# GpSimd's subtractions in two pieces: weights, g of the first batch, maxima of the first pairs

## The chip, the cores and the metric

The kernel runs on one core of one Trainium2 chip. The metric is the device time of one execution in microseconds (us), the median of the runs shown. The engines are named as in the profile: PE (TensorE, matmuls; PEld its weight loads), DVE (VectorE), ACT (ScalarE), POOL (GpSimd) and SP (SyncE, which issues the loads and stores).

## What is computed

Attention over local and global tokens, and behind it a two-layer network with softplus. Batch 8, 8 heads, 512 local and 32 global positions, head dimension 64; the network has 4608 tokens, 512 inputs and 2048 hidden features.

```python
k_all = concat([k_g, k_l]); v_all = concat([v_g, v_l])
out_g = softmax(scale * q_g @ k_all.T) @ v_all
s_ll  = where(|i - j| <= 32, scale * q_l @ k_l.T, -1e9)
out_l = softmax(concat([scale * q_l @ k_g.T, s_ll])) @ v_all
x = concat([out_g, out_l]) as (tokens, heads * dim)
h = x @ w_in
g = max(h, 0) + log1p(exp(-|h|))
out = g @ w_out
```

The weights arrive as 64-bit floats, and the products of the network are made with 32-bit values split in two parts.

## The kernel before

**Two parts.** The attention works on 32 pairs of heads (4 pairs to a batch of the network's input). Pairs 0 to 5 go through a first loop (L674 to L698) step by step: scores on PE, row maximum on DVE (L171, L172), exponential on ACT (L174), reciprocal of the sum on DVE (L180, L181), weighing on POOL (`weigh0`, L186), transposes on PE, copies by ACT (L213, L214), values on PE, and the split of the result (L238, L239). In that loop each step also prepares one weight tile. Pairs 6 to 31 are worked in pieces (`pieces`, L424) that are laid between the network's items of the batch before: `scores`, `block_maxima`, `maxima`, `probs`, `totals`, `values`, `normalise`. Of these, pairs 6, 7 and 8 (m below WIDE, L36) lie in or before batch 0.

**The network.** `moe_items` (L520) lists, batch after batch, `hpart` (PE: four 128-row blocks of x against a weight tile wi, three products each: high by high, low weight by high, high by low), `act` (L545) and `opart` (PE: g against wo, again three products). `act` makes g = e from h: three ACT activations (L548 to L550), one DVE instruction that reads PSUM (L551, called e below), an ACT copy to the high part gh (L554) and a POOL subtraction that leaves the low part gl (L555). `opart` for row block t reads gh twice and gl once, columns 128 t to 128 t + 127 (L563).

**A weight tile.** `abs_w` (ACT, L488) scales the upper words, `bits_w` (DVE, L495, L497 and L500, each from the one before) puts the 32-bit value together, `halves_w` makes the high half by an ACT copy (L505) and the low half by a POOL subtraction (L506). There are 32 such tiles, 16 of each kind (wi and wo). The first 16 are prepared in the first loop (W_PRE, L42).

**The maxima.** `probs` (L371) spreads the block maxima with four DVE transposes (L375) and subtracts them from the scores of both heads on POOL: five subtractions per pair (L378), of 160 and 352 columns a head in the first half of the scores and 32, 384 and 96 in the second. ACT's exponential of that half (L380) follows, then DVE's sums (L384), `totals` with small instructions on 32 partitions (L357 to L361, L389, L390, L393), and at the end `normalise` (L415 to L420).

**Order.** Each engine takes its instructions in the order of its queue. The tile framework draws that order at compile time from a simulated time line (L773), with the program's order as priority and waits where data need them. In the first loop `keep` and `note` (L157, L478) chain the instructions of ACT and DVE, and `mm` those of PE, in the program's order; after it (`tight = False`, L699) PE's chain remains, and DVE's weight work is only kept behind the maxima (L496). POOL's order is left to the framework throughout. Weights after the first 16 are prepared as batch 0 goes on (`weights`, L644, from L704 and L710).

Of the kernel before, what the change touches and what calls it, by code (L numbers as in the profile page):

```python
# [8 lines left out]
F32 = mybir.dt.float32  # L9
# [4 lines left out]
ALU = mybir.AluOpType  # L14
# [21 lines left out]
WIDE = 9  # L36
# [17 lines left out]
def windows(ap2d, start, stride, count, width):  # L54
    base = ap2d[:, start:start + width]
    return bass.AP(base.tensor, base.offset, [list(base.ap[0]), [stride, count], [1, width]])
# [3 lines left out]
def moe_over_global_local_attention(  # L60
# [11 lines left out]
    nc = tc.nc  # L72
# [22 lines left out]
    for o, w, base, sign in ((32, 32, 0, 1), (64, 32, -96, -1), (96, 128, 32, 1), (96, 128, 32, -1)):  # L95
        r = mask0[:, 0, 1, o:o + w]
# [274 lines left out]
    def probs(m, g):  # L371
        s, e = st["s", m], st["e", m]
        mb = pl.tile([P, 2, 416], F32, tag="mb", name=f"mb{m}_{g}", bufs=2)
        for o, k, n in (((0, 1, 8), (256, 7, 5)), ((0, 10, 6), (192, 14, 6)))[g]:
            nc.vector.transpose(mb[:, :, o:o + 32 * n].rearrange("p h (s k) -> p h s k", k=32),  # L375
                                windows(e, k, 21, 2, n).unsqueeze(3).to_broadcast([P, 2, n, 32]))
        for o, q, w in (((0, 0, 160), (160, 64, 352)), ((512, 64, 32), (544, 0, 384), (928, 288, 96)))[g]:
            nc.gpsimd.tensor_tensor(s[:, :, o:o + w], s[:, :, o:o + w], mb[:, :, q:q + w], op=ALU.subtract)  # L378
        s = s[:, :, 512 * g:512 * g + 512]
        nc.scalar.activation(s, s, AF.Exp, scale=0.125)  # L380
        if g == 0:
            st["zt", m] = pl.tile([P, 348], F32, tag="zt", name=f"zt{m}", bufs=2)
            nc.gpsimd.memset(windows(st["zt", m], 0, 36, 3, 4), 0.0)
        nc.vector.tensor_reduce(windows(st["zt", m], 4 + 16 * g, 36, 2, 16), s.rearrange("p h (b k) -> p h b k", k=32),  # L384
                                axis=AX.X, op=ALU.add, apply_transpose=True)
# [38 lines left out]
    def pieces():  # L424
        def piece(*fs):
            def go():
                for f in fs:
                    f()
            return go
        ps = []  # L430
        for m in range(M0, M):
            g0, g1, mx, tot, val = SLOTS.get(m, (None, None, 12 * m + 5, 12 * m + TOT, 12 * m + VAL))
            for g, slot in ((0, g0), (1, g1)) if m in SLOTS else ():
                fs = [lambda m=m, g=g: scores(m, g)]
                if m + 1 < M:
                    fs += [lambda m=m, p=p: load(m + 1, p) for p in ((0,), (1, 2))[g]]
                ps.append((slot, piece(*fs)))
            ps.append((mx, piece(lambda m=m: maxima(m), *[lambda m=m, q=q: probs(m, q) for q in range(2)])))
            ps.append((tot, lambda m=m: totals(m)))
            fs = [lambda m=m: values(m), lambda m=m: normalise(m)]  # L440
            if m + 2 < M:
                fs.append(lambda m=m: load_v(m + 2))
            ps.append((val, piece(*fs)))
        ps.sort(key=lambda t: t[0])
        return ps
# [32 lines left out]
    def note(what, i):  # L478
        if tight:
            keep(what, i)  # L480
        return i
# [9 lines left out]
    def bits_w(kind, k, a):  # L491
        t = raws.pop((kind, k))
        lo32, hi32 = t[:, :, 0], t[:, :, 1]

        i = nc.vector.tensor_scalar(a, a, 3, None, op0=ALU.logical_shift_left)  # L495
        note("dve", i) if tight else after(i, "maxima")  # L496
        note("dve", nc.vector.scalar_tensor_tensor(a, hi32, SIGN, a, op0=ALU.bitwise_and, op1=ALU.bitwise_or))  # L497

        r = lo32 if k < NF - 1 else pl.tile([P, 512], I32, tag="mb", name=f"wlast{kind}", bufs=2)
        note("dve", nc.vector.scalar_tensor_tensor(r, lo32, 29, a, op0=ALU.logical_shift_right, op1=ALU.bitwise_or))  # L500
        return r.bitcast(F32)

    def halves_w(kind, k, r):
        (wi if kind == "wi" else wo)[k] = o = pl.tile([P, 2, 512], F32R, tag=f"{kind}{k}", name=f"{kind}{k}", bufs=1)
        note("act", nc.scalar.copy(o[:, 0], r))  # L505
        nc.gpsimd.tensor_tensor(o[:, 1], r, o[:, 0].bitcast(F32), op=ALU.subtract)  # L506

    def split_w(kind, k):
        halves_w(kind, k, bits_w(kind, k, abs_w(kind, k)))
# [10 lines left out]
    def moe_items():  # L520
# [24 lines left out]
        def act(b, f):  # L545
            ph = g.pop(("ps", b, f))
            e = pl.tile([P, 512], F32, tag="e", name=f"e{b}_{f}", bufs=2)
            nc.scalar.activation(e, ph, AF.Abs)  # L548
            nc.scalar.activation(e, e, AF.Exp, scale=-1.0)  # L549
            nc.scalar.activation(e, e, AF.Ln, bias=one)  # L550
            nc.vector.scalar_tensor_tensor(e, ph, 0.0, e, op0=ALU.max, op1=ALU.add)  # L551
            gh = pl.tile([P, 512], F32R, tag="gh", name=f"gh{b}_{f}", bufs=3)
            gl = pl.tile([P, 512], F32R, tag="gl", name=f"gl{b}_{f}", bufs=3)
            nc.scalar.copy(gh, e)  # L554
            nc.gpsimd.tensor_tensor(gl, e, gh.bitcast(F32), op=ALU.subtract)  # L555
            g[b, f] = (gh, gl)

        def opart(b, f, t):
# [33 lines left out]
        for i, (b, f) in enumerate(tiles):  # L592
            if f == 0 and b > 0:
                items.append((b, 0, 0, lambda b=b: [split_x(b, j) for j in range(4)]))
            if 0 < b < B - 1:
                if f == 0:
                    h = iter(range(NF))
                    for what in ORDER:
                        if what == "H":
                            f = next(h)  # L600
                            items.append((b, 2, 0, lambda b=b, f=f: hpart(b, f, (0, 1))))
                            items.append((b, 2, 0, lambda b=b, f=f: (hpart(b, f, (2, 3)), act(b, f))))
                        elif what == "O":
                            second(done, b)
                            second(done + 1, b)
                            done += 2
                        else:
                            m = next(wide, None)
                            if m:
                                items.append((b, 0, 0, lambda m=m: both_scores(m)))  # L610
                continue
# [3 lines left out]
            w = 0 if b else 4 * f  # L615
            items.append((b, 2, w and w + 2, lambda b=b, f=f: hpart(b, f, (0, 1))))
            items.append((b, 2, w and w + 4, lambda b=b, f=f: (hpart(b, f, (2, 3)), act(b, f))))
            behind = 1 if (b, f + 1) not in tiles or (f == 0 and b > 0) else 2
            upto = halves.index(tiles[i - behind] + (0,)) + (2 if tiles[i - behind][0] < B else 1) if i >= behind else 0
# [54 lines left out]
    for k in range(-2, n + 2):  # L674
        stage(k + 2, 0)

        while k >= n - 2 and pcs[0][0] < min(12 * M0 + 3 * (k - n + 3), START):
            pcs.pop(0)[1]()
        if k == 0:
            key_masks()  # L680
        for at, m, load_0 in ((5, 4, load_q0), (8, 4, load_v0), (8, 5, load_q0), (11, 5, load_v0)):
            if k == at + 1:
                load_0(m)
        if held:
            r = bits_w(*held)
        stage(k + 2, 1)
        stage(k - 2, 5)
        stage(k - 2, 6)
        stage(k, 3)
        stage(k, 4)  # L690
        stage(k + 2, 2)
        if held:
            halves_w(*held[:2], r)
            held = None
        if -1 <= k and wk[1] < W_PRE:
            held = order_w[wk[1]]
            held += (abs_w(*held),)
            wk[1] += 1  # L698
    tight = False  # L699
    if held:  # L700
        halves_w(*held[:2], bits_w(*held))
# [75 lines left out]
```

## Time and profile before

| | us |
|---|---|
| median of 3 runs (984.21 to 985.17) | 984.22 |
| the profiled execution | 983.79 |
| its span | 982.0 |
| PE busy | 946.7 |
| DVE busy | 638.3 |
| ACT busy | 502.8 |
| POOL busy | 434.4 |

The span runs from the first to the last instruction in the trace; the rest of an execution's time lies around it. Busy times are sums over one engine's instructions; the recorded end of matmuls is modelled, so a busy PE is not PE at its best. A row of the order of time gives the start, the length, the engine, the source line, the operation, the tiles (written <- read), the shape and how many were merged; in square brackets the idle time of the engine before it, and what ended it. A row with the line L127 is any matmul, since all go through `mm`; h, o, s and so on tell which. The recorded length of an instruction includes any time that it stands at its engine before its work starts.

### The profile page before, as it was taken

Reading aid. Unit: us, or ns where it says so; the run is one execution under the profiler, and the core shown is the slowest. Engines: PE = TensorE matmul, PEld = TensorE weight load, DVE = VectorE, ACT = ScalarE, POOL = GpSimd, SP = SyncE. Lnnn points to the kernel's source line nnn. Section 1 sums busy time; section 2 is a strip of 40 time slices with the busy share of each in tenths; the row PEclk is TensorE's granted clock in tenths of the full one; section 3 lists DMA queues with packets and bytes.
Section 4 is the critical chain, followed back from the end, with each engine's and each line's share of the span. In section 5 each row is a group of like instructions: output and inputs, shape, how many; then the busy total and the mean of one; then the engine's idle time right before and its main releaser. Section 6 shows DMA issues by size and latency. Waiting matters only on the chain.

```text
span 982.0 us, 14339 instructions
## 1 busy us (share of the span) xinstructions
PE 946.7 (96%) x5236; PEld 763.9 (78%) x5239; DVE 638.3 (65%) x1295; ACT 502.8 (51%) x890; POOL 434.4 (44%) x580
## 2 busy tenths in 40 slices
PE   6797898999999999999999999999999999999998
PEld 3575676778888888888888888888888888888896
DVE  6888959776677866776677677776777676211211
ACT  5786656554445544454464444544454446444553
POOL 5655746534444444253444444444434444222221
PEclk9899899999999999999999999999999999999999
DMA  9824222120112211121112111121112100100000
GB/s 356 319 78 163 85 77 72 43 89 27 43 50 79 64 49 49 50 88 38 50 27 96 37 50 50 55 87 49 50 49 76 50 17 17 50 1 1 12 33 22
DMA packets 34327, 66.21 MB, mean 67 GB/s; under 512 B 7632, under 2 KB 11472, under 8 KB 34256
## 3 DMA queue, kind: packets, MB, share of 16 engines
q1 hardware_dynamic: 33440, 65.19, 20.2%
q8 instruction: 41, 0.67, 0.3%
q14 instruction: 30, 0.25, 0.1%
q10 hardware_dynamic: 816, 0.10, 0.1%
HBM read 55.84 MB, written 9.44 MB: 66 GB/s over the span
## 4 chain that ended last, share of the span: by engine, by line
PE 84%; DVE 9%; ACT 3%; issue 1%; POOL 1%; POOLq 0%; ACTq 0%; DVEq 0%
PE o L127 37%; PE h L127 36%; PE s_ps L127 5%; PE v_ps L127 5%; DVE wbitswi L497 1%; ACT e L174 1%; DVE wiraw L500 1%; DVE wbitswo L497 1%; DVE sums L171 1%; PE s L127 1%; DVE woraw L500 1%; DVE wbitswi L495 1%; DVE wbitswo L495 1%; PE s0g L127 0%; DVE zt L393 0%
## 5 line engine op out<-in xcount | busy, mean ns | idle before, releaser
L127 PE MATMUL h<-xh,wi 128*128 128x512 f32 (+1 forms) x1152 | 347.8, 386 | 10.6 <-DVE e L551 10.6
L127 PE MATMUL o<-wo,gh 128*128 128x512 f32 x1088 | 345.6, 399 | 0.0
L555 POOL TENSOR_TENSOR gl<-e,gh 128x512 fp32r<-128x512 f32 x136 | 180.1, 1324 | 266.2 <-ACT gh L554 235.4
L127 PEld LDWEIGHTS h<-xh,wi 128*128 128x128 f32 x1152 | 214.3, 190 | 57.5 <-DVE e L551 12.3
L127 PEld LDWEIGHTS o<-wo,gh 128*128 128x128 f32 x1088 | 200.3, 188 | 48.2 <-POOL wo L506 0.2
L127 PE MATMUL h<-xl,wi 128*128 128x512 f32 (+1 forms) x576 | 220.6, 383 | 0.0
L127 PE MATMUL o<-wo,gl 128*128 128x512 f32 x544 | 214.6, 394 | 0.7 <-POOL gl L555 0.7
L551 DVE SCALAR_TENSOR_TENSOR e<-h,e 128x512 f32<-128x512 f32 x136 | 92.7, 682 | 183.0 <-ACT e L550 164.7
L548 ACT ACTIVATE e<-h 128x512 f32<-128x512 f32 x136 | 81.0, 596 | 223.4 <-PE h L127 222.9
L378 POOL TENSOR_TENSOR s<-s,mb 128x320 f32<-128x320 f32 (+4 forms) x130 | 138.4, 1097 | 73.3 <-DVE mb L375 73.3
L554 ACT CAST gh<-e 128x512 fp32r<-128x512 f32 x136 | 83.9, 617 | 117.4 <-DVE e L551 117.4
L127 PEld LDWEIGHTS h<-xl,wi 128*128 128x128 f32 x576 | 109.5, 190 | 22.8
L127 PEld LDWEIGHTS o<-wo,gl 128*128 128x128 f32 x544 | 102.3, 188 | 24.8 <-POOL gl L555 1.0
L550 ACT ACTIVATE e<-e,one 128x512 f32<-128x512 f32 x136 | 98.4, 724 | 3.9
L384 DVE TRANSPOSE_TENSOR_REDUCE zt<-s 128x32 f32<-128x1024 f32 x52 | 64.6, 1243 | 48.6 <-ACT s L380 48.5
L549 ACT ACTIVATE e<-e 128x512 f32<-128x512 f32 x136 | 85.9, 631 | 2.9
L380 ACT ACTIVATE s<-s 128x1024 f32<-128x1024 f32 x52 | 55.1, 1059 | 31.1 <-POOL mt L318 25.9
L333 DVE TRANSPOSE_TENSOR_REDUCE mt<-s 128x32 f32<-128x1024 f32 x52 | 64.7, 1244 | 5.0 <-ACT s L322 3.4
L127 PEld LDWEIGHTS s_ps<-raw 64*128 64x128 f32 x728 | 54.6, 187 | 11.4 <-issue 8.9
L354 POOL COPY mt<-mt 32x75 f32<-32x75 f32 x78 | 19.0, 244 | 94.5 <-DVE mt L333 92.4
L127 PE MATMUL s_ps<-raw 64*128 64x192 f32 (+3 forms) x728 | 60.2, 308 | 0.5
L375 DVE STREAM_TRANSPOSE mb<-mt 128x512 f32<-128x512 f32 (+1 forms) x104 | 52.6, 562 | 0.7
(131 smaller groups left out, 860.7 us busy)
## 6 DMA issues: line engine op xcount, KB each, us to landing
raw<-in_qk SPq DMA_DIRECT2D x52, 272.0 KB, 2.8
v<-in_v SPq DMA_DIRECT2D x26, 384.0 KB, 3.1
out<-ot SPq DMA_DIRECT2D x34, 256.0 KB, 2.2
wiraw<-in_w_in SPq DMA_DIRECT2D x16, 512.0 KB, 9.0
woraw<-in_w_out SPq DMA_DIRECT2D x16, 512.0 KB, 8.2
raw<-in_qk SPq DMA_DIRECT2D x26, 224.0 KB, 3.3
v<-in_v SPq DMA_DIRECT2D x6, 512.0 KB, 7.2
raw<-in_qk SPq DMA_DIRECT2D x6, 416.0 KB, 8.4
```

The lines of the kernel that those rows point to most:

```text
L127: order["pe"] = after(nc.tensor.matmul(*a, **k), "pe").ins
L333: order["scores"] = nc.vector.tensor_reduce(windows(st["mt", m], 4 + 16 * g, 36, 2, 16), s.rearrange("p h (b k) -> p h b k", k=32), axis=A ...
L375: nc.vector.transpose(mb[:, :, o:o + 32 * n].rearrange("p h (s k) -> p h s k", k=32), windows(e, k, 21, 2, n).unsqueeze(3).to_broadcast([P ...
L378: nc.gpsimd.tensor_tensor(s[:, :, o:o + w], s[:, :, o:o + w], mb[:, :, q:q + w], op=ALU.subtract)
L380: nc.scalar.activation(s, s, AF.Exp, scale=0.125)
L384: nc.vector.tensor_reduce(windows(st["zt", m], 4 + 16 * g, 36, 2, 16), s.rearrange("p h (b k) -> p h b k", k=32), axis=AX.X, op=ALU.add, a ...
L548: nc.scalar.activation(e, ph, AF.Abs)
L549: nc.scalar.activation(e, e, AF.Exp, scale=-1.0)
L550: nc.scalar.activation(e, e, AF.Ln, bias=one)
L551: nc.vector.scalar_tensor_tensor(e, ph, 0.0, e, op0=ALU.max, op1=ALU.add)
L554: nc.scalar.copy(gh, e)
L555: nc.gpsimd.tensor_tensor(gl, e, gh.bitcast(F32), op=ALU.subtract)
```

## The change

Three kinds of POOL subtraction are issued as two instructions where it was one, each over half of the elements, in the same place of the program: the low half of every weight tile (columns 0 to 255 and 256 to 511), gl of batch 0 (the same columns), and, for pairs 6, 7 and 8, the subtractions of the maxima that are over 160 columns wide (352 and 384), one head at a time.

```diff
         for o, q, w in (((0, 0, 160), (160, 64, 352)), ((512, 64, 32), (544, 0, 384), (928, 288, 96)))[g]:
-            nc.gpsimd.tensor_tensor(s[:, :, o:o + w], s[:, :, o:o + w], mb[:, :, q:q + w], op=ALU.subtract)
+            for h in (slice(0, 1), slice(1, 2)) if m < WIDE and w > 160 else (slice(0, 2),):
+                nc.gpsimd.tensor_tensor(s[:, h, o:o + w], s[:, h, o:o + w], mb[:, h, q:q + w], op=ALU.subtract)
...
         note("act", nc.scalar.copy(o[:, 0], r))
-        nc.gpsimd.tensor_tensor(o[:, 1], r, o[:, 0].bitcast(F32), op=ALU.subtract)
+        for c in (slice(0, 256), slice(256, 512)):
+            nc.gpsimd.tensor_tensor(o[:, 1, c], r[:, c], o[:, 0, c].bitcast(F32), op=ALU.subtract)
...
             nc.scalar.copy(gh, e)
-            nc.gpsimd.tensor_tensor(gl, e, gh.bitcast(F32), op=ALU.subtract)
+            for c in (slice(0, 256), slice(256, 512)) if b == 0 else (slice(0, 512),):
+                nc.gpsimd.tensor_tensor(gl[:, c], e[:, c], gh[:, c].bitcast(F32), op=ALU.subtract)
```

## The prediction

> **What bounds the kernel now.** I read the page first (span, chain by engine), then busy time by stage, then the order of time on DVE and POOL, one beside the other, where PE is not full.
>
> ```profile
> span 982.0 us, 14339 instructions
> PE 84%; DVE 9%; ACT 3%; issue 1%; POOL 1%; POOLq 0%; ACTq 0%; DVEq 0%
> ```
>
> PE holds 84% of the chain that ended last, DVE 9%, POOL 1%. So POOL's own time is worth almost nothing; the question is what POOL does to DVE. The stages, with PE's busy time and granted clock (PEclk):
>
> ```profile
> core 0: us, PE busy (x) PEld busy (x) DVE busy (x) ACT busy (x) POOL busy (x), PEclk, DMA share, GB/s
> 0.00:87.00 87.00, 68.14 (x550) 51.81 (x551) 67.84 (x134) 63.10 (x183) 49.51 (x94) 0.94 0.66 240
> 87.00:101.00 14.00, 7.44 (x26) 5.66 (x25) 13.70 (x21) 7.63 (x14) 10.90 (x11) 0.75 0.30 115
> 101.00:166.00 65.00, 63.94 (x305) 50.40 (x308) 53.36 (x87) 40.30 (x63) 42.80 (x38) 0.98 0.27 88
> 166.00:172.00 6.00, 2.77 (x8) 1.89 (x7) 5.93 (x8) 3.53 (x6) 2.30 (x3) 0.75 0.00 1
> 206.00:982.00 776.00, 771.17 (x4193) 627.95 (x4191) 470.53 (x1003) 368.51 (x593) 309.22 (x416) 1.00 0.15 47
> ```
>
> From 206 on PE is busy 771.17 of 776 us, and the change leaves that part's instructions alone (pairs from 9 on, batches from 1 on): it only moves as a block. PE's slack is in the attention steps (0 to 87), in 87 to 101 and in 166 to 172; in the last two DVE is busy 13.70 of 14.00 and 5.93 of 6.00 us, so DVE is the bound there. Why DVE is so full shows when one of its weight instructions is seen alone and beside a POOL subtraction:
>
> ```profile
> 16.51 0.69 DVE L500 SCALAR_TENSOR_TENSOR wiraw<-wiraw,wbitswi 128x512 int32<-128x512 int32 x1
> 25.02 1.67 DVE L500 SCALAR_TENSOR_TENSOR wiraw<-wiraw,wbitswi 128x512 int32<-128x512 int32 x1
> 24.42 1.73 POOL L506 TENSOR_TENSOR wi<-wiraw,wi 128x512 fp32r<-128x512 f32 x1
> ```
>
> The same L500 takes 0.69 us alone and 1.67 us here, and ends at 26.69, 0.54 after the POOL subtraction's end at 26.15: it does its work after POOL is through. A stall of 0.98 us, set by what is left of one POOL instruction. Its length is what the change cuts.
>
> **The change, part by part.** It adds 54 POOL instructions: 32 for the weights (16 of each kind), 16 for g of batch 0, 6 for the maxima of pairs 6, 7 and 8 (widths 352 and 384, by head). Nothing is moved to another engine or queue, no DMA is added; what reads both pieces (ACT's exponential, PE's products with a whole row) now waits for the second. What a piece costs, from undisturbed POOL groups later in the run (mean ns after the bar):
>
> ```profile
> L555 POOL TENSOR_TENSOR gl<-e,gh 128x512 fp32r<-128x512 f32 x101 | 130.1, 1288 | 187.0 <-ACT gh L554 160.8 <-issue 26.2
> L378 POOL TENSOR_TENSOR s<-s,mb 128x768 f32<-128x768 f32 x22 | 40.8, 1855 | 0.0
> L378 POOL TENSOR_TENSOR s<-s,mb 128x64 f32<-128x64 f32 x22 | 7.1, 323 | 0.0
> ```
>
> (1855 - 323) / 704 columns is 2.18 ns a column, and 323 - 64 x 2.18 leaves 0.18 us per instruction; 512 columns come to 1.30, and the row says 1.288. So 256 columns take an estimated 0.74 us: the first half is there 0.55 earlier than the whole, and the second, with some overlap of neighbours, about 0.14 later. 54 x 0.14 is 7.6 us more of POOL, hidden behind POOL's idle time (49.51 of 87 us busy in the attention); where POOL is full it makes its consumers 0.14 late each.
>
> Whether DVE gets in between two pieces decides everything. Three tiny copies met a run of back-to-back POOL subtractions:
>
> ```profile
> 116.98 1.32 POOL L506 TENSOR_TENSOR wo<-woraw,wo 128x512 fp32r<-128x512 f32 x1
> 118.26 1.31 POOL L506 TENSOR_TENSOR wi<-wiraw,wi 128x512 fp32r<-128x512 f32 x1
> L393 DVE COPY zt<-zt x3: 1146/1255/1268, 115.9 to 118.3; 32x21 f32<-32x21 f32 x3
> ```
>
> Each of the three copies took about one POOL instruction (1146 to 1268 ns), and three copies were done in the time of three subtractions: one DVE instruction slips in at each border. So the pieces halve a stall. But the row also shows the price: a DVE instruction that depends on the one before arrives while the next piece already holds the way. Where a stalled DVE instruction is followed by another that POOL can block, the second half blocks that one, and I count nothing. Where it is followed by one that POOL does not block, 0.55 is gained. The reductions are of that kind (L384 below ran beside five subtractions and took no longer than the mean of all 52; I take L171 and L333 to be alike):
>
> ```profile
> 190.10 6.26 POOL L378 TENSOR_TENSOR s<-s,mb 128x320 f32<-128x320 f32 x5 [2.55 <-DVE mb L375]
> 194.05 1.25 DVE L384 TRANSPOSE_TENSOR_REDUCE zt<-s 128x32 f32<-128x1024 f32 x1
> L384 DVE TRANSPOSE_TENSOR_REDUCE zt<-s 128x32 f32<-128x1024 f32 x52 | 64.6, 1243 | 48.6 <-ACT s L380 48.5
> ```
>
> *Attention, 0 to 87.* Three blocked L500 (the first at 25.02 above, the last at 34.32) are followed by L180, L181 and a reduction: gains. ACT limits what they are worth:
>
> ```profile
> 34.32 1.67 DVE L500 SCALAR_TENSOR_TENSOR woraw<-woraw,wbitswo 128x512 int32<-128x512 int32 x1
> 28.59 0.45 ACT L174 ACTIVATE e<-s,sums 128x224 f32<-128x224 f32 x1 [0.55 <-DVE sums L172]
> 37.60 0.82 DVE L172 TENSOR_SCALAR sums<-sums 128x4 f32<-128x4 f32 x1
> 71.83 0.67 ACT L505 CAST wi<-wiraw 128x512 fp32r<-128x512 f32 x1
> 76.16 0.66 ACT L505 CAST wo<-woraw 128x512 fp32r<-128x512 f32 x1 [1.13 <-DVE woraw L500]
> ```
>
> ACT idled 0.55 us for DVE in such a step, so a gain of 0.55 is just used up; I take 0.45 for each of the three, 1.35. L172 at 37.60, which takes about 0.17 when free, releases the exponentials: 0.55. At 76.16 ACT waited 1.13 for a blocked L500: 0.55. At 71.83 it did not wait, and the same stall there gives nothing. Blocked L497 and L495, each followed at once by its dependent, give nothing. Sum 2.45. Bounds: 0 if every second half finds a victim; 5.5 if all ten stalls that I count in this stage's order of time gave 0.55.
>
> *The first pair's maxima, 93 to 101.*
>
> ```profile
> 94.50 1.96 DVE L497 SCALAR_TENSOR_TENSOR wbitswi<-wiraw,wbitswi 128x512 int32<-128x512 int32 x1
> 96.85 2.29 DVE L500 SCALAR_TENSOR_TENSOR wiraw<-wiraw,wbitswi 128x512 int32<-128x512 int32 x1
> 101.17 1.22 PE L127 MATMUL h<-xh,wi 128*128 128x512 f32 x2 [6.73 <-DVE e L551]
> ```
>
> Against 0.69 alone these lost 1.27 and 1.60, and PE waited 6.73 us for the L551 behind them. Halves of 704 and 768 are about 0.77 and 0.84 shorter, 1.6 at best; but L497, L495, L500 follow each other here, all blockable, so most second pieces find a victim. I take 0.7, between -0.3 (the extra instructions alone) and 1.6.
>
> *PE's second gap, 166 to 172.*
>
> ```profile
> 151.44 1.53 DVE L497 SCALAR_TENSOR_TENSOR wbitswo<-woraw,wbitswo 128x512 int32<-128x512 int32 x1
> 152.89 1.32 DVE L418 TENSOR_TENSOR xa<-xa,lap 128x64 f32<-128x64 f32 x1
> 159.59 1.26 DVE L361 COPY zt<-zt 32x6 f32<-32x6 f32 x1
> 161.37 1.29 DVE L389 TENSOR_SCALAR zt<-zt 32x42 f32<-32x42 f32 x1
> 169.63 1.22 PE L127 MATMUL h<-xh,wi 128*128 128x512 f32 x2 [3.23 <-DVE e L551]
> 169.63 5.49 PE h L127 x12
> 178.29 2.79 PE h L127 x12
> ```
>
> Three small instructions were held over a microsecond each behind g's and the weights' subtractions, and DVE, busy without a break, reached L551 3.23 us late. Halving gives 3 x 0.55 and about 0.35 for the L497 at 151.44: 2.0. Then the gap is 1.2. After it PE's first twelve matmuls took 5.49 instead of 2.79: a restart at low clock (0.75 in this stage), 2.70 lost. What a gap of 1.2 us costs the trace does not show. The neighbour on one side is this one, on the other the gap of 0.73 at 205.39 (below), with twelve per 2.75 after it:
>
> ```profile
> 205.39 0.50 PE L127 MATMUL o<-wo,gl 128*128 128x512 f32 x1 [0.73 <-POOL gl L555]
> 207.98 5.50 PE h L127 x24
> ```
>
> So between 0 and 2.70; I take half, 1.35 saved. Together 3.35, between 0 and 3.23 + 2.70 = 5.93. [...]
>
> *The end of batch 0.* In that last pair PE waited 0.73 for gl; its first two row blocks (L563) need columns 0 to 255 only, so if the wait is by region they start 0.55 earlier, less 0.14 for the weight ahead in POOL's queue: 0.4, between -0.14 and 0.73.
>
> Sum: 2.45 + 0.7 + 3.35 + 0.4 = 6.9 us. The profiled execution took 983.79 us (its span 982.0 and 1.79 around it), 0.43 under the median of 984.22: 983.79 - 6.9 + 0.43 = **977.3 us**.
>
> **The rivals.**
>
> *Hand-over.* Every second piece finds a victim and DVE's total stays; only the stall before ACT's 1.13 wait and the end of batch 0 gain, with L172: 0.55 + 0.55 + 0.4 = 1.5, time 982.7. For it: L393's three stalls in a row. Against: L384, L171 and L333 stand behind several of the stalls.
>
> *Another order (slower).* The order in each queue is drawn at compile time from estimated durations (L773), and after L699 little pins weights against e. New POOL durations can put an L551 behind one more weight chain on DVE between 101 and 169. It decides from the point where L551 comes late enough for PE to restart cold: then a second gap like 166's, 3.23 + 2.70 = 5.93, comes on top, and 166's stays. 984.2 - (2.45 + 0.7 + 0.4) + 5.9 = 986.6. For it: PE has such a gap already. Against: the change alters POOL by a tenth of a microsecond per instruction.
>
> *POOL keeps the way over both pieces.* Then each stall is 0.14 longer; some 20 stalls between 0 and 169 make 2.8, time 987.0. Against: the three copies. [...]
>
> **How the numbers follow.** Forecast 0.57, hand-over 0.22, other order 0.15, POOL keeps the way 0.06. A measurement of this kernel tells about 0.2%, 2 us, from no change. Hand-over is mostly within it (0.18 of 0.22); from the forecast 0.02 falls within. Faster 0.57 - 0.02 + 0.04 = 0.59, same 0.18 + 0.02 + 0.01 = 0.21, slower 0.15 - 0.01 + 0.06 = 0.20. Upper bounds together (5.5 + 1.6 + 5.93 + 0.73 = 13.8) would give 970.5, unlikely all at once: I end the range at 971.5. Upward it takes in hand-over and part of the order case, to 985.5; about 0.2 is left out above and below. The forecast's own range is 973 to 981.
>
> **What would show it.** Right: blocked L500 near 1.1 instead of 1.67; the 20-odd weight stalls halved; PE's gap at 166 under 1.5 with the twelve matmuls after it near 2.8; PE's first h about 2.5 earlier. Wrong: L497 and L500 both stalled where one was (hand-over); a new PE gap ended by e L551 (order); stalls of 1.8 (POOL keeps the way). It is wrong too if ACT, not DVE, paces the steps up to 87 after all.

## The result and the profile after

The changed kernel took 977.94 us (median of four runs, 975.84 to 979.50), the kernel before 984.22 in the runs beside it: a ratio of 0.9937, 95% interval 0.9925 to 0.9949, 6.3 us faster. The predicted time was 977.3. The execution profiled is the slowest of the four, 979.5 us.

The busy times on the page of after:

```profile
PE 948.4 (97%) x5239; PEld 765.0 (78%) x5239; DVE 630.0 (64%) x1295; ACT 502.4 (51%) x890; POOL 451.1 (46%) x634
```

DVE is busy 8.3 us less than before (638.3), POOL 16.7 us more (434.4). DVE's 96 weight instructions (L495, L497 and L500 before, L496, L498 and L501 after) have 3.5 of the 8.3: they took 81.7 us before and take 78.2 after. Before, 23 of them took over 1.0 us, the longest 2.29; after, 32 do, the longest 1.48. So the stalls are shorter, but there are more of them. Here is the order of time of after, DVE in the attention, at the place where the prediction counted "three blocked L500 ... gains" (below L488 the line numbers of after are one to three higher: L500 is now L501):

```profile
22.06 0.18 DVE L181 RECIPROCAL sums<-sums 128x4 f32<-128x4 f32 x1
22.65 1.09 DVE L171 TENSOR_REDUCE sums<-s 128x4 f32<-128x896 f32 x1 [0.41 <-PE s L127]
25.30 1.12 DVE L501 SCALAR_TENSOR_TENSOR wiraw<-wiraw,wbitswi 128x512 int32<-128x512 int32 x1
26.34 0.71 DVE L180 TENSOR_SCALAR sums<-sums 128x4 f32<-128x4 f32 x1
27.08 0.18 DVE L181 RECIPROCAL sums<-sums 128x4 f32<-128x4 f32 x1
31.76 0.18 DVE L181 RECIPROCAL sums<-sums 128x4 f32<-128x4 f32 x1
35.61 0.14 DVE L180 TENSOR_SCALAR sumsg<-sumsg 128x1 f32<-128x1 f32 x1
35.78 0.16 DVE L181 RECIPROCAL sumsg<-sumsg 128x1 f32<-128x1 f32 x1
```

and before:

```profile
22.20 0.18 DVE L181 RECIPROCAL sums<-sums 128x4 f32<-128x4 f32 x1
26.61 0.16 DVE L180 TENSOR_SCALAR sums<-sums 128x4 f32<-128x4 f32 x1
26.80 0.18 DVE L181 RECIPROCAL sums<-sums 128x4 f32<-128x4 f32 x1
31.50 0.18 DVE L181 RECIPROCAL sums<-sums 128x4 f32<-128x4 f32 x1
36.08 0.16 DVE L181 RECIPROCAL sumsg<-sumsg 128x1 f32<-128x1 f32 x1
```

L501 now stands 1.12 us where L500 stood 1.67, as forecast. But the next instruction, L180, an addition on four columns, takes 0.71 instead of 0.16: the second piece holds it. L181 behind it takes 0.18 in both. From L181 to L181 the second of these steps took 4.70 us before (26.80 to 31.50) and 4.68 after (27.08 to 31.76): what the first piece gives, the second takes. The third step is another matter: its L180 adds to one column only (sumsg), took 0.14 beside the second piece, and the step went from 4.58 us (31.50 to 36.08) to 4.02 (31.76 to 35.78), as forecast. The first got longer, 4.60 to 5.02, of which 0.41 is DVE's wait for PE's scores at 22.65.

PE at the gap of batch 0, after:

```profile
167.15 0.73 PE L127 MATMUL h<-xh,wi 128*128 128x512 f32 x2 [2.31 <-DVE e L553]
167.46 1.16 DVE L498 SCALAR_TENSOR_TENSOR wbitswi<-wiraw,wbitswi 128x512 int32<-128x512 int32 x1
168.65 1.13 DVE L501 SCALAR_TENSOR_TENSOR wlastwi<-wiraw,wbitswi 128x512 int32<-128x512 int32 x1
169.78 0.69 DVE L553 SCALAR_TENSOR_TENSOR e<-h,e 128x512 f32<-128x512 f32 x1
```

and before, the two weight instructions behind the gap:

```profile
169.95 1.71 DVE L497 SCALAR_TENSOR_TENSOR wbitswi<-wiraw,wbitswi 128x512 int32<-128x512 int32 x1
171.69 1.66 DVE L500 SCALAR_TENSOR_TENSOR wlastwi<-wiraw,wbitswi 128x512 int32<-128x512 int32 x1
```

The gap is 2.31 us where it was 3.23, and PE goes on at full clock (1.00 from 166.18 to 169.59 us). In this profile, though, PE is slow elsewhere: most of its products of o0g and the first h behind them run at half clock (0.50 from 84.26 to 91.08 us), so the first h starts at 87.85, later than before (87.09). One profile of each kernel is therefore not enough to say where 6 us went; the experiments gave twelve more.

**One table for all.** Four events cut every profile in the same way: PE's first product, DVE's first L333 (pair 6), the first e (L551 before), and the e that ends the gap at 166 (the 11th). In after and before:

```profile
3.92 0.91 PE L127 MATMUL s<-mask,ident 128*128 128x448 bf16 x2 [3.92 <-DVE mask L101]
78.62 1.23 DVE L333 TRANSPOSE_TENSOR_REDUCE mt<-s 128x32 f32<-128x1024 f32 x1
99.16 0.68 DVE L553 SCALAR_TENSOR_TENSOR e<-h,e 128x512 f32<-128x512 f32 x1
166.41 0.68 DVE L553 SCALAR_TENSOR_TENSOR e<-h,e 128x512 f32<-128x512 f32 x1
```

```profile
3.92 0.90 PE L127 MATMUL s<-mask,ident 128*128 128x448 bf16 x2 [3.92 <-DVE mask L101]
79.46 1.24 DVE L333 TRANSPOSE_TENSOR_REDUCE mt<-s 128x32 f32<-128x1024 f32 x1
100.44 0.68 DVE L551 SCALAR_TENSOR_TENSOR e<-h,e 128x512 f32<-128x512 f32 x1
168.90 0.68 DVE L551 SCALAR_TENSOR_TENSOR e<-h,e 128x512 f32<-128x512 f32 x1
173.27 0.68 DVE L551 SCALAR_TENSOR_TENSOR e<-h,e 128x512 f32<-128x512 f32 x1
```

A is from the first product to L333 (after 78.62 - 3.92 = 74.70), B to the first e, C to the 11th e, D1 to the 12th e, D2 to the end of PE's last product. "Slow" counts the stretches of 3.41 us at half clock in 12 to 23 and in 39 to 50 us. The last two columns are medians and ratios, each to the runs of the kernel before that stood beside it (their medians lie between 983.78 and 984.41). The stretches come from one execution each, and that isn't always a typical one: the profile of weights alone is its fastest run (977.40 against a median of 980.58), that of after its slowest (979.50 against 977.94).

| kernel | A | slow | B | C | D1 | D2 | median us | ratio (interval) |
|---|---|---|---|---|---|---|---|---|
| before | 75.54 | 1, 2 | 20.98 | 68.46 | 4.37 | 804.10 | 984.22 | |
| after | 74.70 | 2, 2 | 20.54 | 67.25 | 3.37 | 803.26 | 977.94 | 0.9937 (0.9925 to 0.9949) |
| after again | 73.16 | 2, 1 | 20.38 | 66.72 | 3.37 | 803.34 | 977.41 | 0.9934 (0.9922 to 0.9946) |
| weights alone | 71.51 | 1, 0 | 20.84 | 66.38 | 3.36 | 804.40 | 980.58 | 0.9947 (0.9933 to 0.9960) |
| g alone | 76.10 | 2, 2 | 21.05 | 67.15 | 3.83 | 803.01 | 981.38 | 0.9962 (0.9950 to 0.9975) |
| maxima alone | 76.08 | 2, 2 | 20.56 | 69.40 | 4.37 | 804.42 | 984.48 | 0.9999 (0.9990 to 1.0008) |
| after, maxima whole | 72.93 | 1, 1 | 20.84 | 67.36 | 3.36 | 802.99 | 978.34 | 0.9944 (0.9931 to 0.9956) |
| after without L180 | 71.43 | 1, 1 | 20.53 | 66.94 | 3.37 | 803.30 | 977.12 | 0.9919 (0.9906 to 0.9933) |
| before without L180 | 74.68 | 1, 2 | 21.02 | 68.61 | 4.38 | 804.14 | 982.76 | 0.9986 (0.9977 to 0.9995) |
| weights in quarters | 72.21 | 1, 2 | 19.13 | 67.87 | 5.31 | 802.56 | 978.73 | 0.9950 (0.9936 to 0.9963) |
| extra products, batch 0 | 72.80 | 1, 1 | 20.42 | 67.14 | 3.36 | 803.96 | 978.13 | 0.9941 (0.9930 to 0.9953) |
| extra products, attention | 71.36 | 1, 0 | 20.55 | 66.96 | 3.36 | 803.28 | 975.89 | 0.9922 (0.9909 to 0.9936) |
| first weights in quarters | 70.58 | 1, 1 | 19.08 | 67.78 | 3.37 | 803.57 | 975.17 | 0.9914 (0.9900 to 0.9927) |
| three together | 68.34 | 1, 0 | 19.32 | 67.52 | 3.37 | 803.24 | 972.15 | 0.9876 (0.9859 to 0.9892) |

### The profile page after: what moved, and what is told of

Its sections match the earlier page's. It is cut to its first block, busy times and chain, and to the rows that moved or that the text cites. A ratio compares the mean times of both kernels' runs of the same rounds, so it can differ in the third digit from the quotient of the medians.

```text
span 977.7 us, 14397 instructions
## 1 busy us (share of the span) xinstructions
PE 948.4 (97%) x5239; PEld 765.0 (78%) x5239; DVE 630.0 (64%) x1295; ACT 502.4 (51%) x890; POOL 451.1 (46%) x634
## 4 chain that ended last, share of the span: by engine, by line
PE 85%; DVE 8%; ACT 2%; issue 2%; POOL 1%; DMA 1%; SPq 0%; POOLq 0%; ACTq 0%; DVEq 0%
PE o L127 37%; PE h L127 36%; PE s_ps L127 6%; PE v_ps L127 5%; DVE wbitswo L498 1%; ACT e L174 1%; DVE sums L171 1%; PE s L127 1%; DMA woraw<-in_w_out 1%; DVE woraw L501 1%; DVE wbitswo L496 1%; PE t L127 1%; DVE wbitswi L498 0%; DVE e L553 0%; PE s0g L127 0%
## 5 line engine op out<-in xcount | busy, mean ns | idle before, releaser
L558 POOL TENSOR_TENSOR gl<-e,gh 128x512 fp32r<-128x512 f32 (+1 forms) x152 | 181.8, 1200 | 265.9 <-ACT gh L556 234.8
L379 POOL TENSOR_TENSOR s<-s,mb 128x320 f32<-128x320 f32 (+6 forms) x136 | 139.7, 1062 | 73.0 <-DVE mb L375 73.0
L551 ACT ACTIVATE e<-e 128x512 f32<-128x512 f32 x136 | 85.9, 631 | 2.9
L333 DVE TRANSPOSE_TENSOR_REDUCE mt<-s 128x32 f32<-128x1024 f32 x52 | 64.7, 1245 | 6.2 <-ACT s L322 4.6
```

The costliest lines, as they stand in the source:

```text
L333: order["scores"] = nc.vector.tensor_reduce(windows(st["mt", m], 4 + 16 * g, 36, 2, 16), s.rearrange("p h (b k) -> p h b k", k=32), axis=A ...
L379: nc.gpsimd.tensor_tensor(s[:, h, o:o + w], s[:, h, o:o + w], mb[:, h, q:q + w], op=ALU.subtract)
L558: nc.gpsimd.tensor_tensor(gl[:, c], e[:, c], gh[:, c].bitcast(F32), op=ALU.subtract)
```

## The experiments

### The three parts alone, and one taken away

Weights alone, g alone, maxima alone: the other two loops of the diff go back to the whole subtraction. "After, maxima whole" takes only the maxima's pieces out:

```diff
-            for h in (slice(0, 1), slice(1, 2)) if m < WIDE and w > 160 else (slice(0, 2),):
-                nc.gpsimd.tensor_tensor(s[:, h, o:o + w], s[:, h, o:o + w], mb[:, h, q:q + w], op=ALU.subtract)
+            nc.gpsimd.tensor_tensor(s[:, :, o:o + w], s[:, :, o:o + w], mb[:, :, q:q + w], op=ALU.subtract)
```

> Only the weights' subtractions in two pieces; those of g and of the maxima whole as before. Theory A (a piece halves one stall of DVE, the rest finds the next instruction of DVE that POOL can hold; what shortens the run is the gap at 166 and the cold matmuls behind it): the attention's 0.8 us is all here (PE's first o0g product of pair 0 at about 83.5 instead of 84.3), and of the small stalls ahead of 166 those behind weights are halved (L418, part of L361), so the gap at 166 is about 2.7 instead of 3.23; the restart behind it warm or cold decides between 982.5 and 980. Theory B (the new order of the queues makes the gain): about 984, unless the order of e L551 changes. Theory C (the first half reaching PE and ACT earlier makes the gain): 983.5, since no reader of a weight takes the halves one by one. Forecast 981.5, ratio 0.997.

> Only g of batch 0 in two pieces. Theory A: nothing before 87 (no g there); the stalls behind g between 101 and 169 halve, the gap at 166 shrinks by 0.5 to 1 and the restart behind it may stay warm: 984.2 less 0.5 to 3.5, about 982.5, ratio 0.998. Theory C (the halves reach PE sooner): the 0.73 wait for gl at 205 goes down by 0.4 and the gaps at 108.70 and 127.61 (0.41 and 0.26) go: 983.2. Theory B: 984.2 plus or minus 2, with an exchange in DVE's order before 169.

> Only the maxima of pairs 6 to 8 by head. Theory A: the stalls at 94.50 and 96.85 (1.96 and 2.29) become about 1.2 each, but L495, L497 and L500 follow one another and the second pieces hold those: e L551 0.4 us earlier, 983.8; nothing at 166. If the victims were not there, 1.6 us: 982.6. Theory B: 984.2 plus or minus 2. Forecast 983.8, ratio 0.9995.

> The changed kernel with the maxima of pairs 6 to 8 whole again: weights and g of batch 0 in two pieces. The pieces of the maxima made the stretch from the first L333 to the first e 0.5 us shorter (20.5 against 21.0), but in the kernel with them alone the stretch up to the gap at 166 was 0.9 longer (69.40 against 68.46), with some of DVE's queue in another order. Theory A (the order made that, the pieces gain): here 0.5 slower than the changed kernel, 978. Rival (the extra pieces of POOL cost it in batch 0): 0.4 faster, 977.1. The stretch from the first e to 166 tells: 67.0 or 66.4 (weights alone had 66.38).

The weights give most: A, C and D1 all shrink (C by 2.1, D1 by 1.0). g gives C 1.3, D1 0.5, and D2 1.1. In the profile of g alone, DVE and ACT take their instructions in the same order as before up to 206 us (PE's order is the program's), and it is still 0.4% faster: a gain needs no other order. In the changed kernel DVE's order does differ from before's in several places between 104 and 158 us; what that is worth there wasn't tried apart. The two waits for gl at the end of batch 0, first of weights alone, then of g alone, show the piece reaching PE sooner:

```profile
198.70 0.50 PE L127 MATMUL o<-wo,gl 128*128 128x512 f32 x1 [0.74 <-POOL gl L556]
```

```profile
203.10 0.50 PE L127 MATMUL o<-wo,gl 128*128 128x512 f32 x1 [0.18 <-POOL gl L556]
```

0.56 us less, as forecast by the size of a half (0.55). The maxima are worth 0.4 to 0.5 in B wherever they are split (20.98 to 20.54, 20.84 to 20.5), and nothing measurable in all: alone, C grew by 0.9. In that profile DVE takes a few instructions at 150 to 158 us in another order than before (two of `normalise` ahead of a weight's first instruction, and an e ahead of a reduction of `totals`). But the changed kernel and every other kernel here with the maxima's pieces has the same exchange, and those without these pieces don't. With the weights and g split in halves too, C is 66.7 to 67.25 with it and 67.36 without ("after, maxima whole"). So the expectation that this order made the loss isn't borne out, and why C grew with the maxima alone stays open; one profile for each is thin evidence, and the two times (978.34 and 977.4 to 977.9) can't be told apart. By the medians the three parts come to 3.8 + 3.0 + 0 = 6.8 us, against 6.3 and 6.5 together; with intervals of over 1 us either way these can't be told from a plain sum. In C they don't add: 2.1 and 1.3 alone, 1.1 for weights and g together.

### L180: does the second piece find a victim?

```diff
-        keep("dve", nc.vector.tensor_scalar(t[:, 2, 0:n], t[:, 2, 0:n], 1e-9, None, op0=ALU.add))
         keep("dve", nc.vector.reciprocal(t[:, 0, 0:n], t[:, 2, 0:n]))
```

taken out of the changed kernel, and out of the kernel before (this addition is left out; each sum holds the exponential of its row's maximum, about 1).

> The changed kernel without the addition of 1e-9 to the attention's sums (L180): the sums go to the reciprocal as they are. Theory A: L180 takes the second piece's stall in four of the attention's steps (0.71 instead of 0.16); without it the reciprocal L181 comes next, which POOL didn't hold, and each of these steps ends some 0.5 to 0.7 us earlier, as far as ACT allows: PE's first o0g product at 81.5 to 82.5 instead of 83.5, the run 1 to 2 us faster than the changed kernel, about 976.5. Rival (ACT or the loads pace the steps, L180 was only where the waiting showed): L181 or the next instruction starts no earlier, under 0.3 us gained, 977.7. Rival (the reciprocal is held as well once it stands behind the piece): L181 takes 0.7 instead of 0.16 and nothing is gained.

> The kernel before without the addition of 1e-9 to the attention's sums (L180), all subtractions whole. Theory A (L180 matters in the changed kernel because the second piece hits it): here L180 takes 0.16 us in the crowded steps and runs after POOL is through, so its absence gives 0.2 us a step at most, under 2 us in all before 87 and less at the end: 982.5 to 984. Rival (the step is simply shorter by an instruction with a wait, in either kernel): as much gained as the changed kernel gained by it, 0.8 to 1.8 us: 982.4 to 983.4. The stalls of L500 tell more than the time: 1.67 each in both theories; L181's end in a blocked step, against the start of the step before it.

The reciprocal has line 180 in both. After without the addition:

```profile
21.86 0.17 DVE L180 RECIPROCAL sums<-sums 128x4 f32<-128x4 f32 x1
24.08 2.32 POOL L507 TENSOR_TENSOR wi<-wiraw,wi 128x256 fp32r<-128x256 f32 x2
25.72 0.16 DVE L180 RECIPROCAL sums<-sums 128x4 f32<-128x4 f32 x1
34.47 0.15 DVE L180 RECIPROCAL sumsg<-sumsg 128x1 f32<-128x1 f32 x1
```

Before without it:

```profile
21.95 0.17 DVE L180 RECIPROCAL sums<-sums 128x4 f32<-128x4 f32 x1
35.35 0.15 DVE L180 RECIPROCAL sumsg<-sumsg 128x1 f32<-128x1 f32 x1
```

Reciprocal to reciprocal, the three steps take, in us:

| kernel | first | second | third | sum |
|---|---|---|---|---|
| before | 4.60 | 4.70 | 4.58 | 13.88 |
| after | 5.02 | 4.68 | 4.02 | 13.72 |
| before without L180 | 4.40 | 4.63 | 4.37 | 13.40 |
| after without L180 | 3.86 | 4.92 | 3.83 | 12.61 |

So the pieces alone gave 0.16 in three steps; without the addition they give 0.79. In whole subtractions the addition costs 0.48 in the three steps, in pieces 1.11. The gain isn't in every step, though: it shows in the first, while the second got longer (4.92), with a wait of 0.44 for ACT in it. What the second piece holds is plainer. Four additions on four columns (at 26.34, 31.02, 65.92 and 70.59 in after) met a second piece, and each took 0.70 or 0.71. The two reciprocals on four columns that met one, at 25.72 (POOL is at its two pieces from 24.08 to 26.40) and at 67.16, took 0.16 and 0.17: the piece holds the addition, not the reciprocal. In A at like slow stretches the addition is worth 0.9 us before (75.54 to 74.68) and 1.4 after (72.80 and 72.93 to 71.43). The whole time doesn't separate the theories: by the ratios 1.4 us were gained before, and 1.5 to 1.8 after, with intervals of about 1 us either way.

### Four pieces

```diff
-        for c in (slice(0, 256), slice(256, 512)):
+        for c in (slice(128 * u, 128 * u + 128) for u in range(4)):
```

for all weights, and then for the first 17 only, those up to about 100 us (`w = 128 if len(wi) + len(wo) <= 17 else 256`).

> The weights' subtractions in four pieces of 128 columns (32 weights x 2 more instructions), the rest as in the changed kernel. A piece of 128 is 0.46 us by 0.18 + 128 x 2.18 ns (an estimate from the rows of the subtractions), four are 1.84 against 1.48 for two. Theory A (one DVE instruction per border, each further border finds the next one): L500 0.85 us at a border, then L180, and no second victim once L181 and the reduction come; the step gets no shorter than now by more than 0.25, while POOL gets 0.36 longer for each weight: 977 to 979, not faster than the changed kernel. Rival (the stall is all that counts, and shorter is always better): 2 x 0.28 less on each stalled instruction: 975.5.

> The first 17 weights (those up to 100 us) in four pieces, the others in two, the rest as in the changed kernel. With four pieces throughout, the stretch from the first L333 to the first e (L553) took 19.13 us against 20.4 to 20.5, the attention at the same clock was 1.5 to 2 us shorter, but from the first e to the one that ends the gap at 166 it took 67.87 against 66.7 to 67.25, and the rest 807.87 against 806.7, with PE waiting 1.94 us for a late gl. Theory A (quarters gain where DVE is late, and lose where POOL is): both gains stay and both losses go, 975 to 975.8. Rival (batch 0 swallows what comes earlier, since its weights and x come no earlier): 977.5, with a longer stretch from the first e to 166.

All weights in quarters, the order of time of DVE, then of POOL and PE at 166 to 170:

```profile
25.03 0.84 DVE L501 SCALAR_TENSOR_TENSOR wiraw<-wiraw,wbitswi 128x512 int32<-128x512 int32 x1
25.79 0.43 DVE L180 TENSOR_SCALAR sums<-sums 128x4 f32<-128x4 f32 x1
...
165.99 2.58 POOL L508 TENSOR_TENSOR wo<-woraw,wo 128x128 fp32r<-128x128 f32 x4 [3.28 <-ACT wo L506]
168.53 1.42 POOL L558 TENSOR_TENSOR gl<-e,gh 128x256 fp32r<-128x256 f32 x2
169.31 0.50 PE L127 MATMUL o<-wo,gl 128*128 128x512 f32 x1 [1.94 <-POOL gl L558]
```

Both stalls shrink again (1.12 to 0.84, 0.71 to 0.43). My expectation of "not faster" was right for the whole (978.73) and too low for the parts: B fell by 1.3 us, A is 72.21 with three slow stretches. A part of what gave it back is in the last rows: four pieces of a wo take POOL 2.58 us, gl stands behind them, and PE waits 1.94 us for gl. The 12th e came late too (D1 5.31 instead of 3.37); whether POOL's length or another order of ACT and DVE made that wasn't separated. With quarters only up to 100 us the gains stay and D1 is 3.37 again: 975.17, the forecast being 975 to 975.8. C is 67.8 to 67.9 in both, 0.5 to 1.2 longer than with halves; why wasn't found. In both DVE and ACT take batch 0's first instructions, from 90 to 122 us, in another order than with halves, which wasn't tried apart.

### The clock

In the profiles the granted clock falls to half for whole stretches of 3.41 us. The windows view of before, cut at the borders of such stretches (us, busy time of PE, PEld, DVE, ACT, POOL, then PEclk):

```profile
39.29:42.70 3.41, 1.12 (x13) 0.63 (x9) 2.71 (x7) 3.41 (x12) 1.77 (x5) 1.00 1.04 398
42.70:46.11 3.41, 1.66 (x4) 1.39 (x5) 3.28 (x6) 2.96 (x12) 1.22 (x1) 0.50 0.52 200
46.11:49.53 3.42, 3.42 (x15) 2.91 (x16) 0.64 (x2) 0.79 (x2) 2.99 (x5) 0.50 0.03 7
```

and weights alone, whose borders lie 0.58 us earlier in its span:

```profile
38.71:42.12 3.41, 1.91 (x23) 1.34 (x21) 3.01 (x8) 3.41 (x11) 1.77 (x5) 1.00 1.04 397
42.12:45.54 3.42, 1.83 (x9) 1.63 (x9) 3.08 (x6) 3.20 (x13) 2.41 (x3) 1.00 0.61 232
45.54:48.95 3.41, 3.41 (x37) 2.82 (x37) 2.71 (x4) 2.21 (x6) 2.95 (x6) 1.00 0.58 190
```

PE was busy 1.12 of 3.41 us in the first, and the next stretch is slow; 1.91 and 1.83 in the second, and none is. Over all fourteen profiles the slow stretches of one run lie on one grid, which starts elsewhere in each run, and those up to 215 us are 1, 2 or 3 times 3.41 us long. From 5 to 215 us, every stretch at full clock with PE under 0.50 busy was followed by a slow one but for one at 0.43, and every one at 0.52 or more stayed, except at the o0g products of 64 columns, where 0.65 to 0.81 wasn't enough. The length of the gap doesn't decide: 2.31 us in after stayed at full clock, 2.29 in the same kernel's second profile did not. Its order of time:

```profile
164.20 0.68 DVE L553 SCALAR_TENSOR_TENSOR e<-h,e 128x512 f32<-128x512 f32 x1
164.93 0.74 PE L127 MATMUL h<-xh,wi 128*128 128x512 f32 x2 [2.29 <-DVE e L553]
167.57 0.69 DVE L553 SCALAR_TENSOR_TENSOR e<-h,e 128x512 f32<-128x512 f32 x1
```

and its window behind that gap:

```profile
166.11:169.52 3.41, 3.41 (x10) 2.63 (x9) 2.79 (x4) 3.04 (x5) 3.41 (x5) 0.50 0.00 0
```

The clock records in the traces of before and after fit this: each but the last is a whole multiple of 3.413 us long (3.413, 6.827, 10.240 and more). A stretch with PE busy 0.33 of it (before, 39.29 to 42.70) or 0.48 (after, 12.58 to 15.99) was followed by a slow one.

> The changed kernel itself once more, as the measure for the others of this call. It also tries what the first profiles seem to show: the granted clock is halved only for whole stretches of 3.413 us (or two or three of them), whose borders lie on one grid through a run and on another in the next run, and a stretch is slow if PE was busy for less than about half of the one before it. Theory A (that is the rule): every slow stretch of this run has a length of n x 3.413 us, lies on one grid, and follows a stretch with PE under some 0.55 busy or with the narrow products of o0g; a gap of 2.3 us like that at 165 to 167 then cools in some runs and not in others, whatever the kernel, and the time of one kernel varies by 2 to 4 us. Theory B (the length of the gap alone decides): the gap of 2.31 stays warm again, that of 1.77 before o0g cools again. Time 976 to 980.

The repeat took 977.41, its slow stretches are 3.41 or 6.83 us long and lie on one grid, and the gap of 2.29 cooled where that of 2.31 had not: theory A. But its five times lie within 0.42 us, not 2 to 4.

Two kernels fill gaps with extra products whose results nothing reads. The first, in batch 0, ahead of h of tiles 2 and 12:

```diff
+        def warm(n):
+            t = ps_a.tile([P, 2, 512], F32, tag="a", name=f"warm{n}")
+            for i in range(n):
+                mm(t[:, i % 2], lhsT=wi[0][:, 0, 0:P], rhs=xh[0][:, :512], start=True, stop=True, skip_group_check=True)
...
+            if js[0] == 0 and b == 0 and f in (2, 12):
+                warm({2: 20, 12: 8}[f])
```

The second, in the attention, ahead of the second s0g (`scores0g`, n = 1):

```diff
+            t = ps_h.tile([P, 512], F32, tag="h", name="warm")
+            for _ in range(8):
+                mm(t[:, 0:448], lhsT=ident, rhs=mask0[:, 0], start=True, stop=True, skip_group_check=True)
```

> The changed kernel with 20 extra products ahead of h of tile 2 and 8 ahead of h of tile 12 (batch 0), whose results go to a bank that nothing reads; PE issues them in the gaps of 4.8 to 6.5 us and 2.3 us. They take 0.23 us each: 4.7 and 1.9. Theory A (the slow clock behind the gaps costs time on the path): no slow stretch at 97 to 104 and at 165 to 170; 4.8 us at half clock behind the first gap cost 2.4 us, the second costs 1.7 in about two runs of three: 2.5 to 3.5 us faster than the changed kernel, 974.5 to 975.5, and its runs lie closer together. Rival (DVE paces batch 0 up to the gap at 166, PE's slowness is only filled waiting): the gap at 166 grows by what was gained before it, 977 to 978. Rival (the products don't count as work for the clock): slow stretches as before, 978.

> The changed kernel with 8 extra products of 448 columns (bf16, into a bank that nothing reads) ahead of the second s0g, where PE waits 2.2 us for ACT in the attention. So far the time from PE's first product to the first L333 (pair 6) was 75.5 to 76.1 us with whole weights, each time with two slow stretches at 42 to 50, and 74.70, 72.8 to 73.2 and 71.51 with halves, with two, one and no slow stretch there. Theory A (the halves shorten the idle time ahead of that place, so that it cools less often, and a stretch at half clock there costs 1.3 to 1.5 us of the end): no slow stretch at 42 to 50, first L333 at 71.5 plus or minus 0.4 after the first product in the profile, 975.5 to 976.3 in all, and runs closer together than the changed kernel's 3.7 us. Rival (DVE and ACT pace batch 0 from their own work, what is gained before is lost by 166): the first L333 as early, but 977.5. Rival (the slow stretch is not on the attention's path): first L333 at 73 or later although the clock is full.

In batch 0 the extra products did keep the clock up, and no gain came of it. The window behind the first gap, and PE at its end, in a place where the second profile of after has no gap:

```profile
97.00:105.00 8.00, 5.75 (x24) 4.43 (x24) 8.00 (x12) 4.00 (x6) 5.55 (x9) 1.00 0.00 1
```

```profile
105.08 0.72 PE L127 MATMUL h<-xh,wi 128*128 128x512 f32 x2 [1.46 <-DVE e L560]
```

PE was through sooner, and then waited; DVE is busy 8.00 of 8.00 us: it sets the time there, and the rival of this experiment fits (978.13). This kernel's DVE and ACT also take some instructions from 105 us on in another order than the changed kernel's, so not only the clock differs. D1, without such a difference, says the same of the gap at 166: 3.37 in the second profile of after at half clock (164.20 to 167.57 above), 3.37 in its first at full, and 3.36 here at full. D2 behind it is 803.34 and 803.26 in those two profiles. So the clock behind that gap costs nothing here.

In the attention it does cost: with the extra products A is 71.36 (expected 71.5 plus or minus 0.4) and the time 975.89 (expected 975.5 to 976.3). DVE and ACT keep the changed kernel's order here. The median is 1.5 to 2 us under the changed kernel's two, by the ratios 1.2 to 1.5; the intervals of the ratios overlap, so the stretch A, 1.4 to 1.6 us shorter than in the kernels with one slow stretch in each place, is the stronger evidence. That its runs lie closer together isn't shown: 0.66 us against 3.7 in one series of the changed kernel and 0.42 in the other.

### Three together

Quarters for the first 17 weights, no L180, extra products in the attention.

> Three of the edits together on the changed kernel: the first 17 weights in four pieces, no addition of 1e-9 to the attention's sums (L180), 8 extra products ahead of the second s0g. If the parts add up: up to the first L333 70.58 (four pieces, one slow stretch), less 1.3 (no slow stretch at 42 to 50), less 0.8 to 1.4 (no L180) = 68 to 68.5; from there as in the kernel with four pieces: 973.0 to 973.7 in all. If the attention is by then paced by ACT and the loads: 70, and 974.8.

972.15 us, 0.9876 (0.9859 to 0.9892): 1.2% under the kernel before and 0.6% under the changed kernel. The parts add up, to a little more than forecast. A step of the attention shows what is left:

```profile
25.13 0.83 DVE L504 SCALAR_TENSOR_TENSOR wiraw<-wiraw,wbitswi 128x512 int32<-128x512 int32 x1
25.89 0.16 DVE L180 RECIPROCAL sums<-sums 128x4 f32<-128x4 f32 x1
32.09 0.67 DVE L499 TENSOR_SCALAR wbitswo<-wbitswo 128x512 int32<-128x512 int32 x1 [0.85 <-ACT wbitswo L492]
```

The reciprocal follows L504 at once, and DVE now idles 0.85 us for ACT inside a step. Such waits of its weight work for ACT (L488 before, L492 here) come to 2.5 us from 5 us to the first L333 before, and to 3.7 here, so ACT is likely the next limit; that wasn't tried.

## Why the prediction was right, point by point

**The mechanism** (DVE slips in between two pieces, so a stall halves): right. L501 1.12, L498 1.16 and L501 1.13 stand where 1.67, 1.71 and 1.66 stood. The rival that POOL keeps the way is out: no weight instruction took the 1.8 that it named, the longest took 1.48. But "the 20-odd weight stalls halved" came only in length: with 32 instructions over 1.0 us for 23, most of the stalled time moved on: all weight instructions together lost 3.5 us (81.7 to 78.2). POOL's own price was mis-sized too, 16.7 us instead of 7.6: a weight's two pieces took 2.32 where DVE gets in between (24.70) against 1.73 for the whole, and 1.44 where it does not (36.95).

**Attention, 2.45 of 0 to 5.5.** Where the clock had the same slow stretches (2, 2), A is 74.70 with halves and 76.10 and 76.08 without: 1.4 us. The failed step is "Three blocked L500 ... are followed by L180, L181 and a reduction: gains", for which I took 1.35. Behind the first two the second piece held L180, on four columns (0.71 and 0.70), and neither step got shorter by more than 0.02; behind the third, where L180 has one column, the step gave 0.56. The terms for L172 and for the L500 ahead of ACT's 1.13 wait fit: L172 took 0.43 (at 37.30) instead of 0.82, and the exponentials behind it started 0.40 earlier in their step; the step that ends at 75.36 took 4.02 us (from 71.34), before 4.59 (71.63 to 76.22). 0.56 + 0.40 + 0.57 is 1.5, near the 1.4 measured. What brought A's gain up to the forecast I hadn't counted, so that the size came out is luck: it is the clock. The four kernels with whole weights all had two slow stretches at 39 to 50; of six profiles with halves and nothing added there, one had two, four had one, and one had none. PE waits 1.03 us instead of 1.98 for t0g just ahead, and with the wait behind it (2.21 and 2.06) stands idle 3.2 us there instead of 4.0:

```profile
41.65 0.74 PE L127 MATMUL t0g<-identf,e_g 128*128 128x128 f32 x5 [1.98 <-POOL e L186]
```

```profile
40.96 0.74 PE L127 MATMUL t0g<-identf,e_g 128*128 128x128 f32 x5 [1.03 <-issue]
```

(before, then after.) A stretch less is worth 1.3 to 1.5 us of A (74.70 to 73.16, 72.80 to 71.51), and filling the wait with products, shown above, took the rest of it away. In the profiles with a slow stretch at 42 to 47, a second one followed where PE was busy 0.49 to 0.82 of the first (0.49 to 0.79 with whole weights, 0.68 with all weights in quarters, 0.82 in after), and none where it was busy 0.83 to 0.88. That the shorter wait is the cause was argued from these figures, not tried by itself. All weights in quarters doesn't fit it: PE stands idle only 3.0 us in the two waits there (0.90 and 2.15), and both stretches are slow. Mean A of after, after again, weights alone, maxima whole and extra products in batch 0: 73.0; of before, g alone and maxima alone: 75.9.

**First pair's maxima, 0.7.** 20.98 to 20.54 and 20.38: 0.4 to 0.6. Right.

**PE's second gap, 3.35 = 2.0 + 1.35.** The first term was right in kind: DVE's stalls, C shorter by 1.2 to 1.7 (68.46 to 67.25 and 66.72). The second, "half of cold restart", names the wrong thing. At 166 PE isn't what sets the time; D1 shrank by 1.0 whether PE was slow or not, because the two weight instructions of DVE behind the gap lost half a stall each (1.71 + 1.66 to 1.16 + 1.13 is 1.08). Before, the first of them stood behind a weight's subtraction and the second behind g's; after, both stand behind the two pieces of the weight's, and what meets g's pieces is e, which takes 0.69 as when alone. Together 2.2 to 2.7 instead of 3.35.

**End of batch 0, 0.4.** D2 fell by 0.8 (804.10 to 803.3). 0.54 of it is the shorter wait for gl (0.73 to 0.19 in after, 0.56 as shown with g alone); the rest wasn't traced.

**Sum.** 2.9 + 0.5 + 1.5 + 1.0 + 0.8 = 6.7 by the profiles' means, 6.3 and 6.5 by the two series of times, 6.9 predicted. The sum is closer than its terms: two of them were too large (the L500 of the attention, the gap at 166) and what filled them up (the clock in the attention, D2) wasn't in it. Of the signs named: blocked L500 "near 1.1" came; "gap under 1.5" did not (2.29 and 2.31); "first h about 2.5 earlier" did not in the first profile (87.85, 0.8 later) and came to 1.9 in the second, where PE kept its clock up to 84 (85.17 against 87.09). The hand-over rival was right for the first two L500, and where L496 and L498 follow each other (0.95 and 1.11 at 76.60 and 77.59, before 1.35 and 0.69), but not for the rest. Another order of DVE's queue did come, in the changed kernel too, but no new gap of PE with it: from 101 to 199 us PE waits for an e only once in after, in the gap at 166.

## What to carry to other kernels

Where one engine's instructions hold up another's, as POOL's held DVE's here (L500 1.67 us beside one, 0.69 alone), try cutting them in two: here the same instruction then took 1.12. But only the instruction stream behind the stall says what that is worth: look whether the next instruction can be stalled too, as L180 was (0.71 instead of 0.16), and if it is tiny, whether it is needed at all. Cut finer where the stalled engine paces (quarters took 1.3 us off B), and stop where the cutting engine's own consumers wait (PE waited 1.94 us for gl). Before pricing a slow clock behind a gap, ask which engine ends the stage (D1 was 3.37 us at half clock and at full), and compare profiles only with like slow stretches.

## What was not expected of the hardware

- An addition on 128 x 4 values stood 0.55 us behind a POOL subtraction, its neighbour, a reciprocal of the same size, not at all (0.71 against 0.16, and 0.15 to 0.18 everywhere). The same addition on one column stood behind none: 0.14 beside a second piece, at 35.61 and at 75.19 in after.
- PE at 0.48 busy over one stretch of 3.41 us was slowed in the next (after, 12.58 to 15.99), at 0.54 it was not (weights alone, 42.12 to 45.54); 64-column products at 0.81 busy were (before, 83.66 to 87.07). One stretch at 0.43, not slowed, is the exception. Two profiles of the changed kernel, one with a slow stretch more, differ by 1.5 us in the first 80 us.
